# Gated attention and MLP, one decode step: 512 columns of a weight row moved onto the first six DMA engines, the bias loaded once, and two weight matrices interleaved on TensorE

## The chip, the core and the metric

The kernel runs on one core of a Trainium2 chip. The metric is device time in microseconds (us) for one execution; the time before is the median of three runs. The profile is one further execution that the hardware profiler recorded. In it PE is TensorE's matmul side and PEld its weight loads, DVE is VectorE, ACT is ScalarE, POOL is GpSimd, and SP is SyncE, which here only issues DMAs.

## What is computed

```
g = sigmoid((x * gate_w).sum(-1))                      # x: 2 rows of 576
q = x @ wq                                             # 32 heads of 128
a = softmax(q . k_cache / sqrt(128)) . v_cache  @ wo   # 4096 keys per head; wo: 4096 x 576
b = gelu(x @ w1 + b1) @ w2 + b2                        # w1: 576 x 4608, w2: 4608 x 576
out = g * a + (1 - g) * b
```

All of it is float32. The two caches are 2 x 32 x 4096 x 128 each; with the weights the kernel reads 308.59 MB and writes 4.6 KB.

## The kernel before

**Stages.** First wq and w1 are loaded and multiplied with x (L288 `proj`). Then come 16 steps (L584), each over four heads of one batch row: one 8.4 MB tile of K and one of V. DVE multiplies K by q and sums (L506, L511, L512; POOL helps at L510), ACT takes the exponential (L531), TensorE multiplies with V (L545). At the end come w2 and wo, which TensorE multiplies into one PSUM tile `acc` (L367), and for the last nine rows of wo into `res` (L457, L481); ACT and DVE copy the result out (L477, L486) and SP stores it (L487).

**The ring and the DMA queue.** One SBUF tile `ring` holds three slots of 16384 columns (64 KB per partition). SP issues K, V and the closing weights strictly in the order of `seq` (L100 to L104). A load goes out as soon as the slot that it overwrites is free, so that the DMA engines have work queued nearly all the time. DMAs take eight completion semaphores in turn, so each one also waits until the DMA eight places ahead of it has landed.

**The closing weights.** `LAST` (L66) lists three slots: w2 rows 0 to 27; w2 rows 28 to 35, the piece `wx`, and wo rows 0 to 15; wo rows 16 to 31. "Row r" of w2 here means one of 36 rows that each partition holds (576 columns, 2304 bytes per partition). wo has 32 such rows and goes out in ever smaller DMAs, so that little is left to multiply after the last one.

**The piece wx.** Row 35 of w2 isn't loaded whole over 128 partitions. Its last 288 columns (`DS`) are left out of the w2 DMA (L158), and come through four small DMAs (L155) whose outer dimension is 4 rows (`XE` = 4) with 8 segments of 288 columns each. They put 128 segments into 16 partitions. The matching 128 entries of the hidden vector are spread in the same way with eight tiny matmuls against the identity (L411) into `hx`, and `mlp_x` (L417) multiplies these segments with eight matmuls of 16 rows.

**acc.** Its 576 output columns are two halves of 288 that sit at different partitions (L363 `acc_mm`). [...]

**The bias.** b1 is loaded by ACT's queue into a zeroed tile at two rows of each of four partition groups, one per batch row: the first copy in one DMA early (L221), the second in five pieces after the wq product (L315). The sum at L390 adds it to the hidden row.

**The end.** L601 to L623 write out the order: softmax and attention of the last step, mixed with `mlp_out` (w2), the normalisation (`norm_sum`, `norm_t`, `o_turn`), `mlp_x`, the remaining w2 rows, `wo_out(0, FOLD)` for wo rows 0 to 22 and `last_out` for rows 23 to 31.

Of the kernel before, what the change touches and what calls it, by code (L numbers as in the profile page):

```python
# [8 lines left out]
F32 = mybir.dt.float32  # L9
# [3 lines left out]
P = 128  # L13
# [6 lines left out]
def kernel(  # L20
# [14 lines left out]
    nc = tc.nc  # L35
    B, H, SK, DH = k_cache.shape
    D = x.shape[-1]
# [12 lines left out]
    NG = 4  # L50
# [30 lines left out]
    cp = ctx.enter_context(tc.tile_pool(name="cp", bufs=1))  # L81
# [8 lines left out]
    ps_sm = ctx.enter_context(tc.tile_pool(name="ps_sm", bufs=3, space=bass.MemoryType.PSUM))  # L90
# [8 lines left out]
    kt, vt, wqt, w1t, rows = {}, {}, {}, {}, {}  # L99
# [22 lines left out]
    def slot(n):  # L122
        k = len(held) % SLOTS
        return ring[:, k * SLOT:k * SLOT + n]
# [13 lines left out]
    srcx2 = w2.rearrange("(e c s r) n -> c r e s n", e=XE, c=XC, s=XS)[:, NF - 1, :, :, DS:]  # L138

    def length(w, a, z):  # L140
        return XS * DS if w == "wx" else (z - a) * D - (DS if (w, z) == ("w2", NF) else 0)

    def load_last(m):
        n = sum(length(*q) for q in LAST[m])

        used["e"], used["z"] = len(held) % SLOTS * SLOT + n, (len(held) % SLOTS + 1) * SLOT
        t = slot(n)
        o = 0
        for w, a, z in LAST[m]:
            if w == "wx":  # L150
                xt = t[:XP, o:o + XS * DS]
                rows[w] = xt.rearrange("p (s n) -> p s n", s=XS)
                o += XS * DS
                for c in range(XC):
                    nc.sync.dma_start(xt[c::XC].rearrange("e (s n) -> e s n", s=XS), srcx2[c])  # L155
                continue
            if (w, z) == ("w2", NF):
                nc.sync.dma_start(t[:, o:o + length(w, a, z)], srcs[w][:, a * D:z * D - DS])  # L158
                for r in range(a, z):
                    rows[w, r] = t[:, o + (r - a) * D:o + min((r - a + 1) * D, length(w, a, z))]  # L160
                o += length(w, a, z)
                continue

            ends = (a * D, a * D + DS, a * D + DS + DO, z * D) if (w, z) == ("wo", 32) else (a * D, z * D)
            for u, v in zip(ends, ends[1:]):
                nc.sync.dma_start(t[:, o:o + v - u], srcs[w][:, u:v])
# [41 lines left out]
    b1r = temp(F4)  # L208
# [3 lines left out]
    load()  # L212
    load()

    def load_b1(b, ends):
        to, src = b1r.rearrange("(g q) n -> g q n", g=NG)[:, b], b1.rearrange("(g n) -> g n", g=NG)
        for u, v in zip(ends, ends[1:]):
            nc.scalar.dma_start(to[:, u:v], src[:, u:v])  # L218
# [10 lines left out]
    ident = cp.tile([P, P], F32, name="ident")  # L229
# [9 lines left out]
    for j in range(NPB):  # L239
        t = cp.tile([P, NT * 32 + EB], F32, name=f"p{j}")  # L240
# [86 lines left out]
    for f in range(HG):  # L327
# [10 lines left out]
    nc.vector.tensor_copy(  # L338
        spread.rearrange("p (e c) -> p e c", e=E), row4.unsqueeze(2).to_broadcast([NO, E, PE_])
    )  # L340
    qs = {}
# [20 lines left out]

    def acc_mm(lhsT, rhs, k, start=False, stop=False, lo=0):  # L363
        m = lhsT.shape[-1]
        for s in range(lo, lo + rhs.shape[-1] // DS):
            o = 64 * (k % 2) + 32 * s
            nc.tensor.matmul(  # L367
                acc[o:o + m], lhsT, rhs[:, (s - lo) * DS:(s - lo + 1) * DS], start=start, stop=stop, skip_group_check=True
            )

    g1z = cp.tile([1, 2, 32], F32, name="g1z")
    nc.gpsimd.memset(g1z, 0.0)
# [26 lines left out]
    nc.vector.tensor_mul(t, hb, hb)  # L399
# [6 lines left out]

    load()

    hxps = ps_sm.tile([XP, XS, B], F32, tag="sm", name="hxps")
    for s in range(XS):  # L410
        nc.tensor.matmul(  # L411
            hxps[:, s], ident.rearrange("p (q s) -> p s q", s=XS)[:, s], hg[:, NF - 1], start=True, stop=True
        )
    hx = cp.tile([XP, XS, B], F32, name="hx")
    nc.scalar.copy(hx, hxps)

    def mlp_x():  # L417
        for s in range(XS):
            acc_mm(hx[:, s], rows["wx"][:, s], s, lo=1)

    def mlp_out(lo, hi):
        for r in range(lo, hi):
            acc_mm(hg[:, r], rows["w2", r], r)
# [4 lines left out]
    oP = cp.tile([P, B, 32], F32, name="oP")  # L428

    def o_turn(turn):  # L430
        t = late(B * 32).rearrange("p (b c) -> p b c", c=32)
        for b in range(B):
            nc.vector.transpose(t[:, b], oT[:, b])
        ps = ps_sm.tile([P, B * 32], F32, tag="sm", name="op_t")
        nc.tensor.matmul(ps, turn, t.rearrange("p b c -> p (b c)"), start=True, stop=True)
        nc.vector.tensor_copy(oP.rearrange("p b c -> p (b c)"), ps)

    def wo_out(lo, hi):
        for r in range(lo, hi):
            acc_mm(oP[:, :, r], rows["wo", r], r)  # L440
# [127 lines left out]
    def norm_sum():  # L568
        sums = ps_sm.tile([NO, 1], F32, tag="sm", name="psum")
        nc.tensor.matmul(sums, rs, ones, start=True, stop=True)  # L570
        f = late(1, NO)
        nc.vector.reciprocal(f, sums)
        nc.vector.tensor_mul(f, f, gall)
        nc.vector.tensor_reduce(osum, oall.rearrange("p (r d) -> p d r", d=DH), AX.X, ALU.add)
        nc.vector.tensor_scalar_mul(osum, osum, f[:, 0:1])

    def norm_t():
        ps = ps_sm.tile([P, NO], F32, tag="sm", name="oT_t")
        nc.tensor.transpose(ps, osum, ident[:NO, :NO])
        nc.vector.tensor_copy(  # L580
            oT.rearrange("p b (h e) -> p h b e", e=E), ps.rearrange("p (h b e) -> p h b e", b=B, e=E)
        )

# [68 lines left out]
```

## Time and profile before

| what | value |
|---|---|
| median of three runs | 721.72 us (721.49 to 721.81) |
| the profiled execution | 721.61 us, of which the span from first to last instruction is 719.7 us |
| DMA queue of SP, share of 16 engines over the span | 99.2% |
| DVE busy | 511.8 us (71%) |
| PE busy | 216.2 us (30%) |
| ACT busy / POOL busy | 40.0 us / 145.0 us |

The view of windows gives for each stretch of time the busy time of each engine with the number of its instructions, the granted TensorE clock, and the share of the time in which the 16 DMA engines were busy with packets that began in that stretch; in a short stretch a long packet can push that share above 1. The chain of waits follows the work that ended last backwards. The timeline has start, duration, engine, line, operation, tiles, shapes and count, and in square brackets how long the engine stood idle before and on whom it waited.

### The profile page before, as it was taken

How to read it: one execution, taken by the hardware profiler on the slowest of the kernel's cores; microseconds unless marked ns; L12 is line 12 of the kernel's file. 1: busy time of each engine (PE TensorE's matmuls, PEld its weight loads, DVE VectorE, ACT ScalarE, POOL GpSimd, SP SyncE). 2: the span in 40 equal slices, each digit the busy share in tenths (PEclk: the TensorE clock that was granted, in tenths of full speed). 3: DMA queues.
4: the chain of work that ended last, by engine and by line, in shares of the span. 5: the costliest groups of instructions: out<-in, count | busy, mean ns of one | idle time of the engine just before them, and what ended most of it. 6: DMA issues, size and time to landing. Idle time of an engine off the chain costs nothing.

```text
span 719.7 us, 3881 instructions
## 1 busy us (share of the span) xinstructions
PE 216.2 (30%) x1647; PEld 62.6 (9%) x1647; DVE 511.8 (71%) x136; ACT 40.0 (6%) x156; POOL 145.0 (20%) x35
## 2 busy tenths in 40 slices
PE   0665022040515050404032140505050503113195
PEld 0322000010101010101000010101010100000032
DVE  0004969779695969596969879696959695988910
ACT  0110010100001010101010100001010101010000
POOL 2000130404050403022040404040503122040400
PEclk9977556575756575566657575657575665757599
DMA  9999999999999999999999999999999999999997
GB/s 409 412 446 427 423 452 415 459 416 452 423 437 424 444 426 430 442 430 441 433 431 437 430 426 444 427 437 437 437 427 448 419 434 433 430 441 434 417 424 310
DMA packets 7278, 308.85 MB, mean 429 GB/s; under 512 B 830, under 2 KB 1362, under 8 KB 1628
## 3 DMA queue, kind: packets, MB, share of 16 engines
q1 hardware_dynamic: 7204, 308.55, 99.2%
q8 instruction: 13, 0.21, 0.1%
q10 hardware_dynamic: 56, 0.05, 0.0%
q14 instruction: 5, 0.04, 0.0%
HBM read 308.59 MB, written 0.00 MB: 429 GB/s over the span
## 4 chain that ended last, share of the span: by engine, by line
DMA 47%; DVE 35%; PE 15%; ACT 1%; issue 1%; ACTq 1%; POOL 0%; DVEq 0%; SPq 0%; POOLq 0%
DMA ring<-in_A_k_cache_dram 38%; DVE ring L506 19%; DVE s L511 10%; PE av L545 10%; DVE s L512 5%; DMA ring<-in_B_w_dram 4%; DMA ring<-in_A_wo_dram 3%; DMA ring<-in_gate_w_dram 3%; PE oall L562 2%; PE qps L303 2%; PE acc L367 1%; DVE avs L556 1%; ACTq L218 0%; PE qps L328 0%; ACT p L531 0%
## 5 line engine op out<-in xcount | busy, mean ns | idle before, releaser
L506 DVE TENSOR_TENSOR ring<-ring,q 128x16384 f32<-128x16384 f32 x16 | 275.6, 17225 | 109.1 <-DMA ring<-in_A_k_cache_dram 109.1
L510 POOL TENSOR_TENSOR ring<-ring 128x3968 f32<-128x3968 f32 x16 | 137.0, 8565 | 490.1 <-DVE ring L506 490.1
L545 PE MATMUL av<-ring,p 128*32 128x512 f32 x1024 | 137.5, 698 | 166.9 <-ACT p L531 166.9
L511 DVE TENSOR_REDUCE s<-ring 128x66 f32<-128x8448 f32 x16 | 143.3, 8953 | 1.3
L562 PE MATMUL oall<-avs,pick 128*64 128x512 f32 x16 | 14.8, 1028 | 196.7 <-DVE avs L556 168.3
L512 DVE TENSOR_REDUCE s<-ring 128x62 f32<-128x3968 f32 x16 | 68.4, 4277 | 0.1
L545 PEld LDWEIGHTS av<-ring,p 128*32 128x32 f32 x1024 | 35.1, 127 | 274.8 <-issue 217.8
L531 ACT ACTIVATE p<-s,bs 32x128 f32<-32x128 f32 x64 | 25.5, 398 | 478.9 <-DVE bs L525 477.7
L351 PE MATMUL qb<-qm,spread 64*128 64x512 f32 x8 | 8.3, 1138 | 72.5 <-POOL qm L347 72.5
L390 DVE TENSOR_TENSOR ring<-hps,ring 128x384 f32<-128x384 f32 x3 | 1.7, 559 | 33.3 <-PE hps L303 33.1
L562 PEld LDWEIGHTS oall<-avs,pick 128*64 128x64 f32 x16 | 2.2, 196 | 203.5 <-DVE avs L556 203.5
L367 PE MATMUL acc<-ring,hg 128*2 128x288 f32 x142 | 11.9, 487 | 26.1 <-DMA ring<-in_B_w_dram 26.1
L283 DVE TENSOR_SCALAR gb<-gb 128x2 f32<-128x2 f32 x1 | 0.2, 170 | 24.7 <-ACT gb L282 24.7
L556 DVE TENSOR_TENSOR avs<-av,selr 128x512 f32<-128x512 f32 x8 | 5.5, 682 | 10.6 <-PE av L545 10.6
L303 PE MATMUL hps<-ring 128*32 128x384 f32 x120 | 12.8, 598 | 0.0
L347 POOL TENSOR_TENSOR qm<-qall,mine 64x512 f32<-64x512 f32 x4 | 4.1, 1032 | 41.7 <-ACT qall L330 41.7
L477 DVE COPY ring<-res 2x144 f32<-2x144 f32 x1 | 0.3, 297 | 16.4 <-PE res L457 16.4
L531 ACT ACTIVATION_READ_ACCUMULATOR p<-s,bs 32x1 f32 x64 | 11.8, 184 | 0.0
L303 PE MATMUL qps<-ring 128*32 128x512 f32 x80 | 11.3, 729 | 0.0
L270 PE MATMUL xps<-ident,ring 3*128 3x3 f32 x10 | 1.5, 254 | 24.0 <-DMA ring<-in_gate_w_dram 23.1
L351 PEld LDWEIGHTS qb<-qm,spread 64*128 64x128 f32 x8 | 2.0, 307 | 75.6 <-POOL qm L347 75.6
L353 ACT COPY q<-qb 128x512 f32<-128x512 f32 x4 | 2.3, 586 | 106.3 <-PE qb L351 106.3
(87 smaller groups left out, 74.3 us busy)
## 6 DMA issues: line engine op xcount, KB each, us to landing
ring<-in_B_w_dram SPq DMA_DIRECT2D x2, 4608.0 KB, 34.4
ring<-in_B_w_dram SPq DMA_DIRECT2D x2, 4032.0 KB
ring<-in_A_wo_dram SPq DMA_DIRECT2D x2, 2304.0 KB, 14.9
ring<-in_B_w_dram SPq DMA_DIRECT2D x1, 2160.0 KB
ring<-in_A_wo_dram SPq DMA_DIRECT2D x1, 2016.0 KB
ring<-in_B_w_dram SPq DMA_DIRECT2D x1, 1152.0 KB, 14.7
ring<-in_A_wo_dram SPq DMA_DIRECT2D x1, 1152.0 KB
ring<-in_A_wq_dram SPq DMA_DIRECT2D x1, 1024.0 KB
```

Of the source, the lines that this page charges most:

```text
L303: nc.tensor.matmul(ps[32 * j:32 * j + 32, :width], lhs, ts[c][:, o:o + width], start=(k == 0), stop=last, skip_group_check=True,)
L347: nc.gpsimd.tensor_mul(t, qall.unsqueeze(1).to_broadcast([NO, NQ, DH]), mine[:, u[0]:u[-1] + 1].unsqueeze(2).to_broadcast([NO, NQ, DH]),)
L351: nc.tensor.matmul(ps, spread, t.rearrange("p u d -> p (u d)"), start=True, stop=True)
L367: nc.tensor.matmul(acc[o:o + m], lhsT, rhs[:, (s - lo) * DS:(s - lo + 1) * DS], start=start, stop=stop, skip_group_check=True)
L506: nc.vector.tensor_mul(kt[i], kt[i], qs[i].unsqueeze(1).to_broadcast([P, R, DH]))
L510: nc.gpsimd.tensor_add(t[:, :, :DH2], t[:, :, :DH2], t[:, :, DH2:])
L511: nc.vector.tensor_reduce(st[i][:, HALVED:], kt[i][:, HALVED:], AX.X, ALU.add)
L512: nc.vector.tensor_reduce(st[i][:, :HALVED], t[:, :, :DH2], AX.X, ALU.add)
L531: nc.scalar.activation(p[w, :, e * RB:(e + 1) * RB], st[i][w].rearrange("p (t c) -> p t c", c=RB), AF.Exp, bias=bias[i][w], accum_out=rs[w ...
L545: nc.tensor.matmul(ps[32 * j:32 * j + 32], p[:, 32 * t + EB * (1 - half):32 * t + EB * (1 - half) + 32], vt[i][:, RB * t:RB * (t + 1)].rea ...
L556: nc.vector.tensor_mul(t, avs[i].rearrange("p (r d) -> p r d", d=DH), selr.unsqueeze(2).to_broadcast([P, RB, DH]))
L562: nc.tensor.matmul(oall, pick[:, NO - G - i * G:2 * NO - G - i * G], avs[i].rearrange("p r d -> p (r d)"), start=(i == 0), stop=(i == N // ...
```

## The change

Six edits:

1. wx grows from 288 to 512 columns of row 35 of w2 and is cut for six rows instead of four: four DMAs of 6 x 5 segments (120 segments, 24 partitions), and a fifth DMA of 4 x 2 segments for the remaining eight. The w2 DMA gets shorter by 224 columns: 4096 instead of 4320 per partition.
2. `hx` becomes two tiles, made by five and two matmuls. A segment of 512 columns crosses the border of the two halves of `acc`, so `acc_mm` cuts it into 224 and 288 columns: 14 matmuls instead of 8.
3. wo is divided between the slots at row 15 instead of 16.
4. Of w2's rows 28 to 35, seven are multiplied later: rows 29 and 30 after wo row 7, rows 31 to 35 after wo row 14.
5. b1 is loaded once, to a third row of each group, one piece early and two pieces later; a new DVE addition after the transposition gives it to both batch rows.
6. Four small operations (the copy to `spread`, the scaling of `osum`, the copies to `oT` and `oP`) go from DVE to ACT.

```
-        (("w2", 28, 36), ("wx", 0, 1), ("wo", 0, 8), ("wo", 8, 16)),
-        (("wo", 16, 23), ("wo", 23, 27), ("wo", 27, 30), ("wo", 30, 31), ("wo", 31, 32)),
+        (("w2", 28, 36), ("wx", 0, 1), ("wo", 0, 8), ("wo", 8, 15)),
+        (("wo", 15, 23), ("wo", 23, 27), ("wo", 27, 30), ("wo", 30, 31), ("wo", 31, 32)),
...
-    XE, XC = 4, 4
+    XE, XC, XS, XW = 6, 4, 5, 512
     XP = XE * XC
-    XS = P // XP
+    XN = XP * XS
+    XR, XT = 4, (P - XN) // 4
+    XL = D - XW
...
                 for c in range(XC):
                     nc.sync.dma_start(xt[c::XC].rearrange("e (s n) -> e s n", s=XS), srcx2[c])
+                yt = t[:XR, o:o + XT * XW].rearrange("p (s n) -> p s n", s=XT)
+                nc.sync.dma_start(yt, srcw[XN:].rearrange("(p s) n -> p s n", s=XT))
...
-    load_b1(0, (0, F4))
+    load_b1(0, 1)
...
-    load_b1(1, (0, 232, 464, 696, 928, F4))
+    load_b1(1, FB)
...
-        for s in range(lo, lo + rhs.shape[-1] // DS):
+        hi = lo + rhs.shape[-1]
+        for s in range(NS):
             o = 64 * (k % 2) + 32 * s
+            u, v = max(lo, s * DS), min(hi, (s + 1) * DS)
...
-    hb = ht[:, :, :B]
+    hb = temp(NF * B).rearrange("p (r b) -> p r b", b=B)
+    nc.vector.tensor_add(hb, ht[:, :, :B], ht[:, :, B:B + 1].to_broadcast([P, NF, B]))
...
-    mlp_out(28, NF)
-    wo_out(0, FOLD)
+    mlp_out(28, 29)
+    wo_out(0, 8)
+    mlp_out(29, 31)
+    wo_out(8, 15)
+    mlp_out(31, NF)
+    wo_out(15, FOLD)
```

In the changed file the same code stands 2 to 21 lines further down: the w2 DMA of L158 is L166 there, wx L155 is L157, the other closing loads L166 are L174, `acc` L367 is L380, `res` L457 is L474.

This is SP's queue near its end, first before and then after, with the semaphores that each DMA waits for (DMAHW0 to DMAHW7 are the eight completion semaphores). The shapes are partitions x columns; 4x8x288 is wx, 128x4608 eight rows of wo.

```order
L158 DMA ring<-in_B_w_dram 128x4320 [waits DMAHW5_49,DVE_49]
L155 DMA ring<-in_B_w_dram 4x8x288 [waits DMAHW6_49]
L155 DMA ring<-in_B_w_dram 4x8x288 x3
L166 DMA ring<-in_A_wo_dram 128x4608
L166 DMA ring<-in_A_wo_dram 128x4608 [waits DMAHW7_49]
L166 DMA ring<-in_A_wo_dram 128x4032 [waits DMAHW0_49,PE_49]
L166 DMA ring<-in_A_wo_dram 128x2304 [waits DMAHW1_49,PE_49]
```

And after:

```order
L166 DMA ring<-in_B_w_dram 128x4096 [waits DMAHW2_49,DVE_49]
L157 DMA ring<-in_B_w_dram 6x5x512 x4
L160 DMA ring<-in_B_w_dram 4x2x512 [waits DMAHW3_49]
L174 DMA ring<-in_A_wo_dram 128x4608 [waits DMAHW4_49]
L174 DMA ring<-in_A_wo_dram 128x4032 [waits DMAHW5_49]
L174 DMA ring<-in_A_wo_dram 128x4608 [waits DMAHW6_49,PE_49]
L174 DMA ring<-in_A_wo_dram 128x2304 [waits DMAHW7_49,PE_49]
```

One DMA more stands ahead of wo, so every wo DMA now waits for a DMA one place later than before: the second wo DMA, which waited for w2's first load, waits for its second; the third, for w2's rows 28 to 35.

This is TensorE from the transposition of `osum` to the first rows that go to `res`, before and after (`hg` marks rows of w2, `oP` rows of wo, `hx` the piece wx; "2x288 x16" are eight rows). Of the fourteen wx matmuls after, the last two are shown.

```order
L579 MATMUL oT_t<-ident,ring 128x64
L367 MATMUL acc<-ring,hx 2x288 x8
L435 MATMUL op_t<-ring 128x64
L367 MATMUL acc<-ring,hg 2x288 x15
L367 MATMUL acc<-ring,oP 2x288 x46
L457 MATMUL res<-ring,oP 2x144 x16
```

```order
L380 MATMUL acc<-ring,hx_328 2x224
L380 MATMUL acc<-ring,hx_328 2x288
L452 MATMUL op_t<-ring 128x64
L380 MATMUL acc<-ring,hg 2x288 x2
L380 MATMUL acc<-ring,oP 2x288 x16
L380 MATMUL acc<-ring,hg 2x288 x4
L380 MATMUL acc<-ring,oP 2x288 x14
L380 MATMUL acc<-ring,hg 2x288 x8
L380 MATMUL acc<-ring,hg 2x64
L380 MATMUL acc<-ring,oP 2x288 x16
L474 MATMUL res<-ring,oP 2x144 x16
```

The fifteen w2 matmuls that stood ahead of all of wo are now 2, 4 and 9, the last with 64 columns, and `op_t` stands behind six more wx matmuls.

More of the change, by code (lines that the diff above doesn't have):

```diff
@@ L146, in load_last @@
         used["e"], used["z"] = len(held) % SLOTS * SLOT + n, (len(held) % SLOTS + 1) * SLOT
+        assert n <= SLOT
         t = slot(n)
@@ L150, in load_last @@
             if w == "wx":
-                xt = t[:XP, o:o + XS * DS]
-                rows[w] = xt.rearrange("p (s n) -> p s n", s=XS)
-                o += XS * DS
+                xt = t[:XP, o:o + XS * XW]
                 for c in range(XC):
                     nc.sync.dma_start(xt[c::XC].rearrange("e (s n) -> e s n", s=XS), srcx2[c])
+                o += XS * XW
+                yt = t[:XR, o:o + XT * XW].rearrange("p (s n) -> p s n", s=XT)
+                nc.sync.dma_start(yt, srcw[XN:].rearrange("(p s) n -> p s n", s=XT))
+                o += XT * XW
+                xt = xt.rearrange("p (s n) -> p s n", s=XS)
+                rows[w] = [xt[:, s] for s in range(XS)] + [yt[:, s] for s in range(XT)]
                 continue
             if (w, z) == ("w2", NF):
-                nc.sync.dma_start(t[:, o:o + length(w, a, z)], srcs[w][:, a * D:z * D - DS])
+                nc.sync.dma_start(t[:, o:o + length(w, a, z)], srcs[w][:, a * D:z * D - XW])
                 for r in range(a, z):
@@ L213, with load_b1 @@
     load()
[L215 to L218, printed above, removed]
-    load_b1(0, (0, F4))
+    def load_b1(lo, hi):
+        for m in range(lo, hi):
+            nc.scalar.dma_start(
+                b1r.rearrange("(g q) n -> g q n", g=NG)[:, B, m * FC:(m + 1) * FC],
+                b1.rearrange("(g n) -> g n", g=NG)[:, m * FC:(m + 1) * FC],
+            )
+    load_b1(0, 1)
     for b in range(B):
@@ L337 @@
     spread = cp.tile([NO, P], F32, name="spread")
-    nc.vector.tensor_copy(
+    nc.scalar.copy(
         spread.rearrange("p (e c) -> p e c", e=E), row4.unsqueeze(2).to_broadcast([NO, E, PE_])
@@ L364, in acc_mm @@
         m = lhsT.shape[-1]
-        for s in range(lo, lo + rhs.shape[-1] // DS):
+        hi = lo + rhs.shape[-1]
+        for s in range(NS):
             o = 64 * (k % 2) + 32 * s
-            nc.tensor.matmul(
-                acc[o:o + m], lhsT, rhs[:, (s - lo) * DS:(s - lo + 1) * DS], start=start, stop=stop, skip_group_check=True
-            )
+            u, v = max(lo, s * DS), min(hi, (s + 1) * DS)
+            if u < v:
+                nc.tensor.matmul(
+                    acc[o:o + m, u - s * DS:v - s * DS], lhsT, rhs[:, u - lo:v - lo],
+                    start=start, stop=stop, skip_group_check=True,
+                )
     g1z = cp.tile([1, 2, 32], F32, name="g1z")
@@ L407 @@
     load()
[L409 to L415, printed above, removed]
+    hx = []
+    for n, lo, m in ((XP, 0, XS), (XR, XN, XT)):
+        ps = ps_sm.tile([n, m, B], F32, tag="sm", name=f"hxps{lo}")
+        to_x = ident[:, lo:lo + n * m].rearrange("p (q s) -> p s q", s=m)
+        for s in range(m):
+            nc.tensor.matmul(ps[:, s], to_x[:, s], hg[:, NF - 1], start=True, stop=True)
+        t = cp.tile([n, m, B], F32, name=f"hx{lo}")
+        nc.scalar.copy(t, ps)
+        hx += [t[:, s] for s in range(m)]
     def mlp_x():
-        for s in range(XS):
-            acc_mm(hx[:, s], rows["wx"][:, s], s, lo=1)
+        for s in range(XS + XT):
+            acc_mm(hx[s], rows["wx"][s], s, lo=XL)
     def mlp_out(lo, hi):
@@ L435, in o_turn @@
         nc.tensor.matmul(ps, turn, t.rearrange("p b c -> p (b c)"), start=True, stop=True)
-        nc.vector.tensor_copy(oP.rearrange("p b c -> p (b c)"), ps)
+        nc.scalar.copy(oP.rearrange("p b c -> p (b c)"), ps)
     def wo_out(lo, hi):
@@ L574, in norm_sum @@
         nc.vector.tensor_reduce(osum, oall.rearrange("p (r d) -> p d r", d=DH), AX.X, ALU.add)
-        nc.vector.tensor_scalar_mul(osum, osum, f[:, 0:1])
+        nc.scalar.mul(osum, osum, f[:, 0:1])
     def norm_t():
@@ L579, in norm_t @@
         nc.tensor.transpose(ps, osum, ident[:NO, :NO])
-        nc.vector.tensor_copy(
+        nc.scalar.copy(
             oT.rearrange("p b (h e) -> p h b e", e=E), ps.rearrange("p (h b e) -> p h b e", b=B, e=E)
```

5 lines of the change are left out of this document (3 added, 2 removed).

## The prediction

> **What bounds the kernel now.** I read the page first, then the view of windows, then the chain of waits and the timeline of the end.
>
> ```profile
> span 719.7 us, 3881 instructions
> DMA packets 7278, 308.85 MB, mean 429 GB/s; under 512 B 830, under 2 KB 1362, under 8 KB 1628
> q1 hardware_dynamic: 7204, 308.55, 99.2%
> q8 instruction: 13, 0.21, 0.1%
> q10 hardware_dynamic: 56, 0.05, 0.0%
> ```
>
> One queue, SP's (q1), keeps the 16 DMA engines busy for 99.2% of the span. No other engine is near that. The windows show where the remaining share goes (the last two columns are the DMA share and GB/s):
>
> ```profile
> 30.00:60.00 30.00, 24.48 (x178) 8.49 (x174) 0.00 (x0) 3.01 (x13) 1.12 (x2) 0.77 1.01 436
> 60.00:680.00 620.00, 154.68 (x1048) 38.57 (x1040) 504.38 (x113) 31.57 (x125) 140.01 (x19) 0.62 1.00 433
> 680.00:712.00 32.00, 27.61 (x317) 9.46 (x319) 5.05 (x13) 2.39 (x9) 0.00 (x0) 0.92 0.99 424
> 712.00:713.50 1.50, 0.87 (x16) 0.27 (x14) 0.00 (x0) 0.40 (x1) 0.00 (x0) 1.00 0.96 391
> 713.50:714.00 0.50, 0.50 (x24) 0.44 (x20) 0.00 (x0) 0.00 (x0) 0.00 (x0) 1.00 0.95 374
> 714.00:714.50 0.50, 0.50 (x24) 0.35 (x16) 0.00 (x0) 0.00 (x0) 0.00 (x0) 1.00 0.78 303
> 714.50:715.00 0.50, 0.22 (x8) 0.00 (x0) 0.00 (x0) 0.00 (x0) 0.00 (x0) 1.00 0.59 214
> 715.00:715.50 0.50, 0.14 (x8) 0.13 (x11) 0.00 (x0) 0.00 (x0) 0.00 (x0) 1.00 0.52 194
> 715.50:716.00 0.50, 0.50 (x24) 0.40 (x16) 0.00 (x0) 0.00 (x0) 0.00 (x0) 1.00 0.46 158
> 716.00:716.50 0.50, 0.50 (x22) 0.17 (x12) 0.00 (x0) 0.00 (x0) 0.00 (x0) 1.00 0.47 119
> 716.50:717.00 0.50, 0.50 (x15) 0.24 (x12) 0.10 (x1) 0.06 (x1) 0.00 (x0) 1.00 0.00 0
> ```
>
> From 30 to 712 us the share stays at 0.99 to 1.01: no gap is there to close. The end is ragged: in engines out of 16 the shares are 15.2, 12.5, 9.4, 8.3, 7.4, 7.5, then none. So about four engines have finished by 714.5, four more by some 715, and eight carry the rest to about 716.5. The unused part from 713.5 to 716.5 is (0.05 + 0.22 + 0.41 + 0.48 + 0.54 + 0.53) x 0.5 = 1.1 us of all sixteen. That is what perfect levelling of the same bytes would give.
>
> ```profile
> 695.27 20.04 DMA ring<-in_A_wo_dram
> 715.31 0.04 issue
> 715.36 1.56 PE res L457 x36
> 716.92 0.28 DVE ring L477
> ```
>
> The chain says the same: 20 us of wo transfers, then TensorE takes up the last rows as they land, and copies follow. TensorE itself waits for DMA at each piece:
>
> ```profile
> 697.79 2.10 PE L367 MATMUL acc<-ring,hx 16*2 16x288 f32 x16
> 699.82 0.43 PE L435 MATMUL op_t<-ring 128*128 128x64 f32 x2
> 705.82 2.12 PE L367 MATMUL acc<-ring,oP 128*2 128x288 f32 x32 [1.58 <-DMA ring<-in_A_wo_dram]
> 710.57 2.11 PE L367 MATMUL acc<-ring,oP 128*2 128x288 f32 x28 [2.63 <-DMA ring<-in_A_wo_dram]
> 712.73 0.40 ACT L446 COPY ring<-acc 128x288 f32<-128x288 f32 x1 [17.24 <-PE acc L367]
> 714.29 0.43 PE L467 MATMUL res<-ring,fold 128*2 128x144 f32 x8
> 716.67 0.48 PE L481 MATMUL res<-ring,oP 128*2 128x72 f32 x8
> ```
>
> The last matmuls end at 717.15, and 2.55 us of copying and storing stand behind them to the end of the span at 719.7. So the time is the last engine's last byte plus a fixed tail. The question is only how many bytes the last engine carries.
>
> **The transfers.** 433 GB/s over 16 engines are 27.1 GB/s for one, or 27.1 KB per us. The w2 DMA shrinks by 224 columns: 8 partitions x 224 x 4 = 7168 bytes less on each of the 16 engines, 0.26 us. In exchange wx grows. Before, it was 4 DMAs of 8 segments x 1152 bytes per engine, 36.9 KB or 1.36 us on four engines. After, it is 4 x 5 x 2048 = 41.0 KB (1.51 us) on six engines, and 4.1 KB more (0.15 us) on the first four. Net of the w2 part: engines 0 to 3 get 8.2 KB more in wx and 7.2 KB less in w2, +0.04 us; engines 4 and 5, +1.51 - 0.26 = +1.25 us; engines 6 to 15, -0.26 us. The bias takes 4.6 KB off each of the four engines that its four-row DMAs use: -0.17 us. Engines 0 to 3 come to -0.13 us.
>
> That a four-row DMA keeps to engines 0 to 3 and a six-row one to engines 0 to 5 I take from the change's own wording; no row says it. What the trace has is that issuing one differs:
>
> ```profile
> L155 SPq DMA_DIRECT2D ring<-in_B_w_dram x4: 618/624/805, 682.5 to 684.7; - x4
> L158 SPq DMA_DIRECT2D ring<-in_B_w_dram x1: 328/328/328, 681.8 to 681.8; - x1
> ```
>
> SP takes 0.62 us for one of 36 KB and 0.33 us for one of 2160 KB. The Trainium skill, "DMA: Bandwidth & Descriptors", section "Why a DMA increments its semaphore by 16 and not by 1", says that a DMA runs on the largest number of engines, up to 16, that divides the outermost dimension on both sides, on the lowest-numbered ones, and that the issuer itself writes the semaphore steps of the others. The longer issue agrees with that; the engine numbers no view here can show.
>
> Which engine ends last? Eight end together. Four may be those with wx, 1.36 us heavier. The others must be late for another reason, and one is in sight:
>
> ```profile
> q1 hardware_dynamic: 1696, 14.77, 87.3%
> q8 instruction: 3, 0.05, 0.5%
> ```
>
> In the window from 680 to 720 us three fetches of TensorE's instructions took 0.5% of 16 engines x 40 us, 3.2 us, thus about 1.07 us each on whichever engine they hit. All the program has 13. So the late eight are, as I read it, four engines with wx and four that were hit more often, and the early eight hold engines 4 and 5. Then the late engines outside wx win 0.26 us and those with wx 0.13 us. I take 0.26, because with or without wx the eight lie within half a microsecond, and q10's 56 packets (six bias DMAs of four rows, each row with a completion packet, make 48 of them) also become 32, all on engines 0 to 3. The bounds: 0.13 us if an engine with wx is the very last, up to 0.5 if small packets count more than their bytes. Engines 4 and 5 at +1.25 us land at some 715.3 to 716.3, still ahead of the last.
>
> The skill has a rule that speaks against this edit. The same page, section "Rules for kernel authors", says to put a dimension that is a multiple of 16 outermost, since a smaller one confines the DMA to that many engines. By it the 262 KB belong on all sixteen, 0.60 us for each, and the change, which confines 115 KB more, would cost time. The shares of 0.59 down to 0.47 decide against it here: bytes on an engine that is already idle at 715 cost nothing.
>
> **The extra DMA and the later waits.** One more DMA means about 0.6 us more of SP, and the wait one place later:
>
> ```profile
> 682.52 2.83 SPq L155 DMA_DIRECT2D ring<-in_B_w_dram  x4
> 685.40 15.23 SPq L166 DMA_DIRECT2D ring<-in_A_wo_dram  x9
> SPq L166 <- DMA ring<-in_B_w_dram: 8.1, 2, 4.7
> ```
>
> The second wo DMA now waits for w2's second load, as the third did before, and the third for rows 28 to 35; each goes out 4 to 5 us later than before. Queued behind them on SP are the smaller wo pieces only. Cover: wo rows 0 to 7 alone are 147 KB per engine, 5.4 us, and the engines are still on w2 and wx when the second is issued. I cost it at nothing; without that cover an engine would stand up to 4.7 us.
>
> **TensorE's tail.** wx becomes 14 matmuls, 28 records. Bounds: at the pace of the 16 (2.10 us, 0.13 each) 3.7 us, at that of the wo rows (2.12 for 32) 1.9 us. So `op_t` comes up to 1.6 us later, near 701.4, and wo rows 0 to 7 with it. Rows 29 to 35 of w2 are 13 matmuls, 26 records, 1.7 us by the pace of the wo rows, and fall into the idle 1.58 and 2.63 us. The eight rows that now come before row 23 need 32 records, 2.12 us, from about 710.3: `acc` is complete near 712.4, as now. Cover if all this is late: `acc` is needed for L467 at 714.29, the copy ends at 713.13, so 1.2 us are free. Cost 0. On the path: 0.
>
> **ACT, DVE, bias.** One DVE addition more and some copies on another engine:
>
> ```profile
> L399 DVE TENSOR_TENSOR ring<-ring 128x72 f32<-128x72 f32 x1 | 0.2, 235 | 0.0
> L580 DVE COPY oT<-oT_t 128x64 f32<-128x64 f32 x1 | 0.2, 225 | 1.5 <-PE oT_t L579 1.5
> L506 DVE TENSOR_TENSOR ring<-ring,q 128x16384 f32<-128x16384 f32 x16 | 275.6, 17225 | 109.1 <-DMA ring<-in_A_k_cache_dram 109.1
> ```
>
> 0.24 us at 67 us, where DVE waits 109.1 us for K over 16 steps: hidden. The copies at the end lie ahead of wo rows 0 to 7, with the slack above. Three bias DMAs fewer also shift the semaphores of the early loads; at a share of 1.01 there is no gap to close there.
>
> **Sum.** -0.26 us on the last byte, nothing elsewhere: 721.61 - 0.26 = 721.35 for the profiled execution. It lies 0.11 us below the median of the runs shown, so 721.46 by the median; I say 721.4. A measurement of this kernel can tell about 0.2%, 1.44 us, from no change.
>
> **Rivals.**
> - *Better levelling (chance 0.08).* The late engines are just those with wx, and their small packets cost more than I count. For it: eight end together. The ceiling is the 1.1 us above: 720.6. Even that is under 0.2%; with noise 0.03 for more.
> - *Engines 4 and 5 are not early (0.10).* For it: no view names an engine. Against it: by the shares, if the four with wx are among the late eight, eight of the other twelve have finished by some 715. If one of them is among the eight, it ends 1.25 us after the present last: 722.9, or 723.2 with 0.3 us for packets. It is what the skill's rule above would come to.
> - *The six rows do not spread over six engines (0.05).* This is the one that ends slower. If two engines take a six-row DMA, they carry 123 KB of wx instead of 41, +3.0 us on engines that are among the last: 721.6 - 0.1 + 3.0 = 724.5; on three, +1.5 and 723.0. It decides, against 0.2%, where one of the last engines gets 39 KB (1.44 us) more than now. For it: this trace holds no six-row DMA. Against it: the four-row ones, which the rows show going by without trouble, differ in nothing but the count.
> - *An instruction fetch at the end (0.05).* The last one lies in the window from 716 to 717:
>
> ```profile
> q8 instruction: 1, 0.02, 8.9%
> ```
>
> TensorE's stream is 5 matmuls longer ahead of the tail (6 more for wx, one less for `hx`), so that fetch comes some 0.4 us earlier (ten of the 36 records in the 1.56 us of the chain) and could hit an engine that still carries wo: +1.07 - 0.26, 722.4.
>
> **How the numbers follow.** The forecast has 0.72, its own range 720.9 to 721.7. The range 720.6 to 722.8 takes in better levelling, the fetch and most of the forecast's noise; it leaves out late engines 4 and 5 and the worse spread, 0.15. Faster by over 0.2% (below 720.28): 0.03. Slower (above 723.16): six rows on two engines (0.04) and the dear end of late engines 4 and 5 (0.03), 0.07. The rest, 0.90, is no change.
>
> **What would show it.** Right: the shares from 713.5 to 716.5 fuller, about ten engines busy at 715, none after 716.3; L481 starting near 716.4; the 2.55 us behind it unchanged. Idle time of TensorE ahead of the wo pieces near 0 at rows 8 to 14. Wrong: a share of 0.1 to 0.4 that reaches beyond 717 (a few engines overloaded: two or three engines for the rivals with six rows), a share well under 1 between 695 and 712 (the later waits), or L446 starting after 713.9 (TensorE).

## The result and the profile after

The changed kernel took 723.06 us (median of 20 executions, 721.92 to 723.71), the kernel before 721.56 us beside it (20 executions, 721.41 to 722.33). The ratio is 1.0020 with a 95% interval of 1.0014 to 1.0026: slower by 1.0 to 1.9 us. The executions of before lie within 0.9 us, those of after over 1.8 us. That spread is part of the answer, so below the times of a kernel are given as a distribution as well as by a median. One single execution of 994 us, of the kernel with the old bias and row 35 on four engines, is left out.

The profiled execution of after took 723.66 us, 2.05 us more than that of before. Its page still has one queue that is busy all the time, with the smaller bias traffic on q10:

```profile
span 721.7 us, 3898 instructions
q1 hardware_dynamic: 7216, 308.55, 99.1%
q8 instruction: 13, 0.21, 0.1%
q10 hardware_dynamic: 32, 0.03, 0.0%
```

The windows of the end (the last two columns are the DMA share and GB/s):

```profile
714.00:714.50 0.50, 0.50 (x12) 0.06 (x4) 0.00 (x0) 0.00 (x0) 0.00 (x0) 1.00 1.00 401
714.50:715.00 0.50, 0.12 (x4) 0.00 (x0) 0.00 (x0) 0.31 (x1) 0.00 (x0) 1.00 0.77 311
715.00:715.50 0.50, 0.26 (x11) 0.23 (x15) 0.00 (x0) 0.09 (x1) 0.00 (x0) 1.00 0.83 325
715.50:716.00 0.50, 0.50 (x28) 0.43 (x20) 0.00 (x0) 0.00 (x0) 0.00 (x0) 1.00 0.69 259
716.00:716.50 0.50, 0.50 (x24) 0.29 (x12) 0.00 (x0) 0.00 (x0) 0.00 (x0) 1.00 0.64 224
716.50:717.00 0.50, 0.14 (x8) 0.00 (x0) 0.00 (x0) 0.00 (x0) 0.00 (x0) 1.00 0.45 150
717.00:717.50 0.50, 0.21 (x8) 0.20 (x12) 0.00 (x0) 0.00 (x0) 0.00 (x0) 1.00 0.23 83
717.50:718.00 0.50, 0.50 (x24) 0.35 (x18) 0.00 (x0) 0.00 (x0) 0.00 (x0) 1.00 0.18 58
718.00:718.50 0.50, 0.50 (x19) 0.23 (x12) 0.00 (x0) 0.00 (x0) 0.00 (x0) 1.00 0.06 17
```

Two things are to be seen. The fall begins later: at 714.0 to 714.5 the share is 1.00 where before had 0.78, so all engines are late, not only the last. And it ends in a tail: 0.45, 0.23, 0.18 and 0.06 in engines are 7, 4, 3 and 1, where before kept 7.5 engines until 716.5 and then none. TensorE, ScalarE's copy of `acc` and the chain follow the last byte as before (the fourteen matmuls of wx are 28 records, two for each, as the eight of before were 16):

```profile
698.74 2.10 PE L380 MATMUL acc<-ring,hx 24*2 24x224 f32 x28
706.60 3.26 PE L380 MATMUL acc<-ring,oP 128*2 128x288 f32 x26 [2.10 <-DMA ring<-in_A_wo_dram]
712.50 2.12 PE L380 MATMUL acc<-ring,oP 128*2 128x288 f32 x32 [1.13 <-DMA ring<-in_A_wo_dram]
718.60 0.48 PE L498 MATMUL res<-ring,oP 128*2 128x72 f32 x8
```

```profile
714.69 0.40 ACT L463 COPY ring<-acc 128x288 f32<-128x288 f32 x1 [13.23 <-PE acc L380]
```

```profile
697.31 19.93 DMA ring<-in_A_wo_dram
717.24 0.04 issue
717.29 1.55 PE res L474 x36
718.84 0.28 DVE ring L494
```

The last matmuls end at 719.08, and 2.6 us of copying and storing stand behind them, as they did (2.55 us). All 2.05 us were therefore lost by the DMA engines before 719. When, the group of the K multiplications shows, since nearly each of them waits for the last engine of its K tile. First and last start stand in the row; this is before and then after:

```profile
L506 DVE TENSOR_TENSOR ring<-ring,q x16: 17224/17226/17226, 70.4 to 651.1; 128x16384 f32<-128x16384 f32 x16
```

```profile
L523 DVE TENSOR_TENSOR ring<-ring,q x16: 17208/17225/17226, 74.0 to 652.0; 128x16384 f32<-128x16384 f32 x16
```

The last K tile is complete 0.9 us later, before row 35 or any of wo is loaded. So some of the loss arises ahead of it, and the rest of the 2.05 us shows only at the end. The early part is visible on ScalarE. Its timeline around the bias, before and then after (ACTq is ACT issuing DMAs; in brackets its idle time and what ended it):

```profile
39.79 2.65 ACTq L218 DMA_DIRECT2D ring<-in_B_b_dram  x5
42.49 0.89 ACT L322 COPY ring<-ident 128x8 f32<-128x8 f32 x8 [2.36 <-issue]
```

```profile
38.61 1.05 ACTq L226 DMA_DIRECT2D ring<-in_B_b_dram  x2
47.51 0.90 ACT L332 COPY ring<-ident 128x8 f32<-128x8 f32 x8 [8.56 <-DMA ring<-in_B_b_dram]
```

The two late bias pieces are issued 1.2 us earlier than the five, but ScalarE now stands idle for 8.56 us ahead of the eight small copies behind them, until these pieces have landed. In the program's order the wait is there in after and not in before, where it stood on the activation of the hidden vector (L402), at a place where the bias had long come:

```
before  L322 COPY ring<-ident 128x4x2 [waits Pool_49]
before  L402 ACTIVATE ring<-ring 128x72 [waits DMAHW2_49,DMAHW3_49,DMAHW1_49,DMAHW4_49,DMAHW0_49,DVE_49]
after   L332 COPY ring<-ident 128x4x2 [waits DMAHW1_49,DMAHW0_49,Pool_49]
after   L417 ACTIVATE ring<-ring 128x72 [waits DVE_49]
```

The copies neither read nor write the bias; why the program puts the wait there I can't say from the runs. On the copies hangs TensorE's query product, behind that, on the same engine, the product with w1, and on that the slot that V's first tile overwrites. SP's issue of that V tile and its wait, before and then after:

```profile
61.43 0.33 SPq L130 DMA_DIRECT2D ring<-in_A_v_cache_dram  x1
SPq L130 <- PE hps L303: 13.3, 1, 13.3
```

```profile
66.07 0.33 SPq L130 DMA_DIRECT2D ring<-in_A_v_cache_dram  x1
SPq L130 <- PE hps L313: 18.0, 1, 18.0
```

V goes out 4.6 us later. That matters because of what is queued ahead of it. By the completion events in the trace the sixteen engines finish the first K tile from 68.4 to 70.2 us, in both kernels. Before, the next 8.4 MB had been queued 7.0 us ahead of the first of these times; after, 2.4 us ahead. And the V tile's completions, as a mean over the engines, follow those of K after 19.32 us before and after 19.75 us after. So the engines were without queued work for 0.43 us each in the mean. The shares of the windows can't show it, since at this place they count 64 KB packets by their start.

### The profile page after: what moved, and what is told of

Its sections match the earlier page's. It is cut to its first block, busy times and chain, and to the rows that moved or that the text cites. A ratio compares the mean times of both kernels' runs of the same rounds, so it can differ in the third digit from the quotient of the medians.

```text
span 721.7 us, 3898 instructions
## 1 busy us (share of the span) xinstructions
PE 218.4 (30%) x1657; PEld 64.1 (9%) x1657; DVE 510.9 (71%) x133; ACT 41.1 (6%) x161; POOL 145.0 (20%) x35
## 4 chain that ended last, share of the span: by engine, by line
DMA 47%; DVE 35%; PE 14%; ACT 2%; issue 1%; ACTq 0%; POOL 0%; SPq 0%; DVEq 0%; POOLq 0%
DMA ring<-in_A_k_cache_dram 39%; DVE ring L523 19%; DVE s L528 10%; PE av L562 9%; DVE s L529 5%; DMA ring<-in_A_wo_dram 3%; DMA ring<-in_gate_w_dram 3%; ACT p L548 2%; DMA ring<-in_B_w_dram 2%; PE hps L313 2%; PE qps L313 1%; DMA ring<-in_B_b_dram 1%; PE qps L338 1%; PE zps L289 0%; DVE ring L409 0%
## 5 line engine op out<-in xcount | busy, mean ns | idle before, releaser
L562 PE MATMUL av<-ring,p 128*32 128x512 f32 x1024 | 139.0, 704 | 161.2 <-ACT p L548 161.2
L529 DVE TENSOR_REDUCE s<-ring 128x62 f32<-128x3968 f32 x16 | 68.4, 4276 | 0.0
L380 PE MATMUL acc<-ring,hg 128*2 128x288 f32 (+1 forms) x142 | 13.6, 505 | 25.8 <-DMA ring<-in_B_w_dram 25.8
L380 PE MATMUL acc<-ring,oP 128*2 128x288 f32 x92 | 8.0, 475 | 3.3 <-DMA ring<-in_A_wo_dram 3.2
```

Source lines behind the costliest of these rows:

```text
L380: nc.tensor.matmul(acc[o:o + m, u - s * DS:v - s * DS], lhsT, rhs[:, u - lo:v - lo], start=start, stop=stop, skip_group_check=True,)
L529: nc.vector.tensor_reduce(st[i][:, :HALVED], t[:, :, :DH2], AX.X, ALU.add)
L562: nc.tensor.matmul(ps[32 * j:32 * j + 32], p[:, 32 * t + EB * (1 - half):32 * t + EB * (1 - half) + 32], vt[i][:, RB * t:RB * (t + 1)].rea ...
```

## The experiments

Theory A: the loss comes from the late bias pieces, by way of ScalarE's copies and V's first load. Rival B: the early shift is hidden, and all the loss is the ragged end. The first four kernels set them against each other.

**Late bias pieces behind the first query unit.**

```
     nc.scalar.dma_start(b2r, b2[None, :])
-    load_b1(1, FB)
...
     q_unit(0)
+    load_b1(1, FB)
```

> The changed kernel with the two late bias pieces issued behind the first q tile instead of ahead of the small ACT copies at L332. Theory A (the late pieces hold ACT for 8.6 us, so the first V tile is issued 4.6 us later and the DMA engines run empty at 68 us; part of the 1.1 us by which the sixteen engines are later on the average): V's first load goes out near 61.5 us again, and the time falls by 0.4 to 1.1 us to 722.0 to 722.7. Theory B (all of the loss is the end: an engine that got wx is a late one): no change, 723.1.

**Row 35 as before, all else changed.**

```
-    XE, XC, XS, XW = 6, 4, 5, 512
+    XE, XC, XS, XW = 4, 4, 8, 288
```

> The changed kernel with wx as before: 288 columns over four engines. Theory A: still 722.0 to 722.7, above before by 0.4 to 1.1 us, with V's first load at 66 us. Theory B: 721.5, as before, since the overloaded engine is gone.

**The kernel before with the bias edit alone.**

```
-    load_b1(0, (0, F4))
+    load_b1(0, 1)
...
-    load_b1(1, (0, 232, 464, 696, 928, F4))
+    load_b1(1, FB)
...
-    hb = ht[:, :, :B]
+    hb = temp(NF * B).rearrange("p (r b) -> p r b", b=B)
+    nc.vector.tensor_add(hb, ht[:, :, :B], ht[:, :, B:B + 1].to_broadcast([P, NF, B]))
```

> The kernel before with the bias edit alone (one copy, one early piece and two late ones, the addition after the transposition). Theory A: ACT waits some 8 us at L324 and the time rises by 0.4 to 1.1 us, to 722.0 to 722.7. Theory B: 721.5, no change.

**The changed kernel with the bias as before** (the reverse of that diff).

> The changed kernel with the bias loaded as before. Theory A: the time falls by 0.4 to 1.1 us from 723.1, to 722.0 to 722.7, what is left being the end; V's first load near 61.5 us. Theory B: no change, 723.1.

Here are all runs of ten executions or more, these and the later ones; those with fewer come further down. The mean of before beside them was 721.59 to 721.64 throughout, and none of its executions was above 722.34.

```
kernel                                 executions  above 722.4  median   mean    ratio to before (95%)
after                                      20          18       723.06  723.05   1.0020 (1.0014 to 1.0026)
after, late bias behind query unit         11           5       721.60  722.12   1.0007 (0.9998 to 1.0016)
after, row 35 on four                      11           8       723.13  722.85   1.0017 (1.0008 to 1.0026)
before, bias edit alone                    11           5       722.29  722.43   1.0012 (1.0003 to 1.0021)
after, bias as before                      11           6       722.62  722.23   1.0009 (1.0000 to 1.0018)
after, late bias, row 35 on four           11           0       721.74  721.80   1.0002 (0.9993 to 1.0011)
after, old bias, row 35 on four            10           0       721.60  721.64   1.0000 (0.9991 to 1.0009)
before, row 35 on six alone                11           6       722.63  722.30   1.0009 (1.0000 to 1.0018)
after, bias whole and early                11           4       722.02  722.15   1.0007 (0.9998 to 1.0016)
before, five engines, 384 columns          11           2       721.60  721.79   1.0003 (0.9994 to 1.0012)
before, four engines, 384 columns          11           1       721.69  721.81   1.0003 (0.9994 to 1.0012)
before, six engines, 256 columns           11           1       722.06  722.04   1.0006 (0.9997 to 1.0015)
after, late bias, five engines, 384        11           0       721.65  721.70   1.0001 (0.9992 to 1.0010)
```

B falls: with row 35 as before the loss stays (723.13), and the bias edit by itself costs 0.80 us in the mean. A holds as far as it goes; its 722.0 to 722.7 misses two of the four medians, 721.60 with the late bias and 723.13 with row 35 on four. In the run with the late bias behind the query unit ScalarE does not wait and V goes out at 55.5, with 12.9 us in hand instead of 2.4:

```profile
39.72 0.90 ACT L331 COPY ring<-ident 128x8 f32<-128x8 f32 x8
55.54 0.33 SPq L130 DMA_DIRECT2D ring<-in_A_v_cache_dram  x1
L523 DVE TENSOR_TENSOR ring<-ring,q x16: 17224/17226/17227, 70.0 to 650.9; 128x16384 f32<-128x16384 f32 x16
```

In the one with the bias edit alone both come back:

```profile
48.00 0.90 ACT L324 COPY ring<-ident 128x8 f32<-128x8 f32 x8 [8.59 <-DMA ring<-in_B_b_dram]
64.87 0.33 SPq L130 DMA_DIRECT2D ring<-in_A_v_cache_dram  x1
```

That profiled execution had 3.4 us in hand; its V tile followed after 19.33 us, nothing lost, and it took 721.62 us. The one with row 35 on four engines had 2.4 us in hand (issued at 65.92), followed after 19.93 us and took 723.23. So by these three profiles the edge lies between 2.4 and 3.4 us of lead. The times of the bias edit alone spread from 721.62 to 723.61, as they would if its executions fall on both sides of that edge; no profile shows one of its long ones.

The profile with row 35 on four engines answers one thing more. Its end has a tail like that of after:

```profile
716.50:717.00 0.50, 0.50 (x24) 0.29 (x20) 0.00 (x0) 0.00 (x0) 0.00 (x0) 1.00 0.27 95
717.00:717.50 0.50, 0.50 (x24) 0.42 (x24) 0.00 (x0) 0.00 (x0) 0.00 (x0) 1.00 0.16 53
718.00:718.50 0.50, 0.50 (x16) 0.28 (x12) 0.04 (x1) 0.00 (x0) 0.00 (x0) 1.00 0.12 34
```

Its last load's completions spread over 4.23 us, those of after over 4.18, of before over 3.22. So the tail goes with the late V load and is no sign of the six engines. How a mean loss of 0.6 us at 88 us becomes 1.5 us on the last engine the trace doesn't tell, since it names no engine.

A is not all, however. With the bias mended in either way about half of the executions are back at 721.2 to 721.9 us, and the other half stand 1.2 to 1.4 us above (by the groups' medians); with the late bias there is nothing between (721.25, 721.41, 721.43, 721.51, 721.59, 721.60 and 722.50, 722.75, 722.90, 722.90, 723.43). ScalarE doesn't wait in either kernel and V goes out early enough (55.5 and 60.0), so it isn't the early shift that makes the second group. Theory C puts it to row 35's 512 columns on six engines, theory D to the rest of the change: the kept-back rows, ScalarE's copies, wo's boundary at 15.

**Late bias behind the query unit and row 35 on four** (both diffs above).

> The changed kernel with the two late bias pieces issued behind the first query unit and with row 35 of w2 as before (288 columns on four engines). Theory A (the loss is V's first load, issued 4.6 us late): as in the run with only the bias moved, most executions at 721.4 to 721.7. The open remainder is a second group of times some 1.2 us higher that the runs with the late bias behind the query unit and with the bias as before both had. Theory C (that group comes from row 35's 512 columns on six engines): no second group here, all times within 721.3 to 722.0 and a median of 721.5. Theory D (it comes from the kept-back rows, the copies on ScalarE or wo's second boundary): the second group stays, with some 3 to 6 of 11 times at 722.4 or above.

**Bias and row 35 as before; the order, the copies and the boundary changed.**

> The changed kernel with the bias as before in six pieces and row 35 of w2 as before: what is left of the change is the order of rows 29 to 35 behind wo's rows 7 and 14, the copies moved to ScalarE and wo's boundary at row 15. Theory C: one group of times, 721.3 to 722.0, median 721.5. Theory D: a second group of times at 722.4 to 723.0 with some 3 to 6 of 11 times.

**The kernel before with row 35 on six engines and wo's boundary at 15** (these parts of the change's diff alone).

> The kernel before with row 35's 512 columns of w2 on six engines and wo's boundary at row 15, everything else (bias, order on TensorE, copies on VectorE) as before. Theory C: two groups of times, some 5 of 11 at 722.4 to 723.0 and the others at 721.3 to 722.0. Theory D: one group at 721.3 to 722.0. By my prediction's levelling alone it would be 0.1 to 0.3 us faster than before.

**The changed kernel with the bias loaded once, whole and early.**

```
-    load_b1(0, 1)
+    nc.scalar.dma_start(
+        b1r.rearrange("(g q) n -> g q n", g=NG)[:, B], b1.rearrange("(g n) -> g n", g=NG)
+    )
...
-    load_b1(1, FB)
```

> The changed kernel with the bias loaded once and whole, early, in one DMA at the place of the first piece, so that nothing late is left for ScalarE's eight copies to wait for. Theory A: V's first load is issued at 61.5 us or earlier and no engine runs dry at 68 us; the lower group of times at 721.3 to 721.6. Theory B (all of the loss is at the end): 722.4 to 723.4 as in the changed kernel. Theory C and D both leave a second group at 722.4 to 723.0 here, since the six engines, the order and the copies are all in it.

C holds and D falls: without the six engines there is no second group (21 executions, though two of those with the late bias reach 722.03 and 722.30), with them there is, in all four kernels. The bias whole and early is the least clear of these, with 722.02 and 722.11 between the groups; its V load goes out at 55.7 us. What is left of the change when bias and row 35 are put back (kept-back rows, copies, boundary) costs nothing: 721.60 against 721.58. Added to before one by one, the two costs make up the whole: the bias edit alone has a mean of 0.80 us above before, the six engines alone of 0.66 us, the whole change of 1.44 us. Taken out of the change one by one, they are 0.93 and 0.20 us. A mean of eleven is uncertain by some 0.25 us, so the runs don't tell these two accounts apart, and the close sum is partly luck.

Why half of the executions? Two more runs of the kernel with row 35 on six were meant to catch a profile of the second group.

> The kernel before with only row 35's 512 columns on six engines, once more, for a profile of the higher group of its times. Two accounts of that group. Theory E (an engine with a piece of row 35 is a late one in such an execution): in a profile at 722.6 or above the DMA share falls below 1 from 714 us on and 0.1 to 0.4 of it lasts until 717 us, as in the changed kernel, while the loads up to 690 us end within 0.2 us of the lower group's. Theory F (all engines are late, by longer packets somewhere): the stages before 690 us end 1 us later and the share at the end falls as steeply as in the lower group, only later.

> As the run before this one; the higher group held 6 of its 11 times, so one of two should show it. Theory E: share of 0.1 to 0.4 until 717 us or later. Theory F: a steep end, later by some 1 us.

Both fell into the lower group (721.56 and 721.39 us), so no profile shows the second group undisturbed by the bias, and E against F was not settled in this way. Two other kernels changed the count of engines and the width.

**Five engines, 400 columns; and four engines, 432 columns** (the first in the kernel before with wo's boundary at 15, the second with the order and copies of after too).

```
-    XE, XC, XS, XW = 6, 4, 5, 512
+    XE, XC, XS, XW = 5, 4, 6, 400
```

```
-    XE, XC, XS, XW = 4, 4, 8, 288
+    XE, XC, XS, XW = 4, 4, 8, 432
```

> The kernel before with 400 columns of row 35 on five engines instead of 288 on four, and wo's boundary at row 15. If it is the fifth engine that is late in the higher group, that group stays here, some 1.0 us above the lower one, with about half of the times; if only the sixth is, there is one group at 721.3 to 722.0. Theory F (longer packets everywhere, nothing to do with which engine) has one group here or two without regard to the count of engines.

> The changed kernel with the bias as before and 432 columns of row 35 on the first four engines, so that these four carry half as much again as before and no fifth or sixth engine carries any. Theory E: one group of times and no second one at +1.2 us, since the four are never late; the four early engines get 144 columns x 32 rows x 4 bytes or 18 KB more each, which their lead of some 1.5 us before row 35 takes up: 721.3 to 722.2. If it is the width of row 35's part and not the engine that makes the second group, it stays.

They took 730.64 and 725.67 us (medians of four and five executions), as nothing had led me to expect, and said nothing on the question. With these widths SP got a new wait ahead of row 35, for loads that were still running (the row of the five engines, then that of the four):

```profile
SPq L157 <- DMA ring<-in_B_w_dram: 11.9, 1, 11.9
694.00:696.00 2.00, 2.00 (x35) 0.93 (x37) 1.19 (x4) 0.00 (x0) 0.00 (x0) 1.00 0.00 0
```

```profile
SPq L157 <- DMA ring<-in_B_w_dram: 7.0, 1, 7.0
694.00:696.00 2.00, 2.00 (x26) 0.85 (x28) 0.86 (x3) 0.43 (x1) 0.00 (x0) 1.00 0.05 20
```

For 2 us the DMA engines have nothing or next to nothing to do. Widths of 256, 288, 384 and 512 columns don't bring this wait, so the next kernels keep to those.

They test an account (theory G) that came from the trace's records; theory H stands for the other accounts, by the width of the piece or by its form. The records of q8, TensorE's instruction fetches, have durations that repeat with a period of eight. In the kernel with six engines: 926, 960, 962, 949, 880, 880, 944, 938 ns, then 921, 961, 967, 953. I read this as eight engines taken in turn. The completion times of one load's sixteen parts fit that. Those of the load at 687 us, after ten fetches, make groups of 8, 6 and 2 (us after the first):

```
0.00 0.21 0.22 0.58 0.68 0.72 0.76 0.94 | 1.22 1.27 1.35 1.36 1.43 1.47 | 2.85 2.92
```

By that reading eight engines were hit by no fetch, six by one and two by two. The last two stand clearly apart; the border between the eight and the six (0.94 and 1.22) is drawn to fit the count. By the means of the groups a fetch would cost its engine 0.8 to 1.5 us. By the end there were twelve, hence four engines hit once and four twice. If row 35's engines lie outside the eight, then by their completions in the last load three sorts are left: never hit and without row 35, hit once, and all the rest. The first two sorts count 4 and 4 with four engines (before), but with six engines 3 and 3:

```
before      0.00 0.44 0.71 0.86 | 1.48 1.56 1.57 1.59 | 2.33 and later
six engines 0.00 0.23 0.27      | 1.39 1.44 1.51      | 2.23 and later
```

Three left unhit means that only five of the six with row 35 are outside the eight. The sixth is one of the eight; here it had been hit once. In an execution in which it is one of the four that are hit twice it would end some 1.3 us later, and that would be half of them, if the turn began at each of the eight with equal chance.

The other profiles bear the counts out: 3 and 3 also in the five others with 512 columns on six engines and no wait for the bias (in two of them with a less clear border behind the second 3), 4 and 4 in the four others with 288 or 384 columns on four engines in which V lost nothing. The equal chance they don't bear out. The first durations (934, 926, 884, 879 ns) are places in the same series of eight, and by them the eighteen profiles begin at only four of the eight places. From each of these four the engine behind that of 947 ns (880 to 888 ns) is hit once by the twelfth fetch. If that is the sixth, it explains why all seven profiles with six engines and no wait for the bias are of the lower group. After begins at the same place as before and as two of these seven. That the turn begins elsewhere in the executions that are not profiled is not shown.

**Five engines with 384 columns, four with 384, six with 256** (in the kernel before, boundary at 15).

```
-    XE, XC, XS, XW = 6, 4, 5, 512
+    XE, XC, XS, XW = 5, 4, 6, 384
```

> The kernel before with 384 columns of row 35 on five engines, and wo's boundary at row 15; no added wait on SyncE. Theory G: if the sixth engine is the one that also brings instructions, one group of times, 721.3 to 722.0; if the fifth is, two groups some 1.2 us apart as with six engines. Theory H: two groups, or one, whatever the engine, as in the run with four engines of 384 columns.

> The kernel before with 384 columns of row 35 on four engines, and wo's boundary at row 15. An engine with 32 rows of 1536 bytes has some 2.1 us for them by the records of 1152 (51 ns) and 2048 bytes (84 ns), 0.4 us more than with 288 columns, which these four early engines can take. Theory G: one group, 721.3 to 722.0. Theory H by width: a second group some 0.6 us higher; H by the form in 24 and 4 rows: one group.

> The kernel before with 256 columns of row 35 on six engines, and wo's boundary at row 15. Theory G: the engine that is hit twice has 20 rows of 1 KB (some 47 ns each, 1.0 us) instead of 20 of 2 KB (1.7 us) to bear, so the second group stays but lies only some 0.5 us above the lower one. Theory H by width: no second group; H by form: the second group at 1.2 us above as before.

G's forecasts come out but for a few strays. With six engines and 256 columns there are two groups that lie closer, 721.56 to 721.79 (five) and 722.06 to 722.35 (five, and one at 723.17): their medians are 0.63 us apart, where some 0.5 was expected and 1.2 had been measured with 512 columns. With five engines nine of eleven lie at 721.40 to 721.83, with four and the same width ten of eleven at 721.63 to 721.80, so it is the sixth engine that brings the second group, and the width sets how far off it lies. Five engines have the fifth DMA and the later waits of wo too, so these don't make the group either. The last loads agree: five engines leave 3 unhit and 4 hit once (0.00 0.22 0.40 | 1.52 1.67 1.72 1.83 | 1.97 and later). Two and one stray executions at 722.7 to 722.9, where the second group would be, stay unexplained. What is shown is that the sixth engine costs the time in about half of the executions; that instruction fetches are the reason is argued from the records and from these forecasts, and no profile shows it at work.

**Both causes mended:** the changed kernel with the late bias behind the query unit, and 384 columns on five engines.

> The changed kernel with the late bias pieces issued behind the first query unit and with 384 columns of row 35 on five engines; the kept-back rows, the copies on ScalarE and wo's boundary at row 15 stay as changed. If the two causes are all of the loss: one group of times at 721.3 to 721.8 with at most a stray one above, a median of 721.4 to 721.7, no measurable difference from before. If something else of the change costs time: a median of 722.0 or more, or a second group. That it is faster than before by over 0.2% (720.2 or less) neither account expects.

721.65 us, one group of 721.33 to 722.06: no difference from before that can be measured (0.9992 to 1.0010). So the two causes account for the loss as far as the runs can tell, and what is left of the change brings nothing. No version beat the kernel before.

## Why the prediction was wrong

- **The bias edit, costed as hidden.** This is the step that failed: "Three bias DMAs fewer also shift the semaphores of the early loads; at a share of 1.01 there is no gap to close there". It looked for a gain and at SP's semaphores. It left out ScalarE, on whose own queue the late pieces are issued: the wait for them moved from L402, where it was free, ahead of the eight copies, and the query product, w1's product and V's first load are queued behind these. A share of 1.01 says that no gap is there; it doesn't say how much delay the queue bears. That was 7.0 us of lead, and 4.6 us of it went. Measured: +0.80 us in the mean for the bias edit alone (1.0003 to 1.0021).
- **Engines 4 and 5 as early ones.** The rival "Engines 4 and 5 are not early", with a chance of 0.10 and 722.9 us, came true for one engine and in about half of the executions: the upper group of the kernels without the bias cost lies around 722.7 to 722.9 (medians of four kernels). That the whole change came out near this number, at 723.06, is chance, since there the bias cost is in it. I had counted late engines in one profile, and, if theory G is right, in one profile the fetches' turn begins at one place. The mean cost was +0.66 us. A DMA with six rows does run on six engines: each of the four has six completions in the trace, which lie within 0.7 us where row 35 alone was changed. The rival with two or three engines falls.
- **The gain of 0.26 us.** The lower group with six engines has a median of 721.55 us, five engines with 384 columns 721.60, before 721.6. By these medians levelling has brought 0.1 us at most; where the rest of the 0.26 us went no run tells.
- **The rule that I weighed against the trace.** The Trainium skill, "DMA: Bandwidth & Descriptors", section "Rules for kernel authors", advises against an outermost dimension below 16. I set it aside since bytes on an idle engine cost nothing. With four or five engines that held (1.0003 for either with 384 columns); with six it did not (+0.66 us), by theory G since the sixth is not an early engine in each execution.
- **What was right.** The tail behind the last matmul stayed at 2.6 us. The 28 records of wx took 2.10 us, near the lower of the two bounds. The kept-back rows, ScalarE's copies and the boundary at 15 cost nothing (1.0000, 0.9991 to 1.0009), and with the later waits of wo the kernel with both causes mended has no loss either (1.0001, 0.9992 to 1.0010). The second wo load went out 4.5 us later, near the 4 to 5 forecast, the third 6.7 us. That TensorE would hardly wait ahead of rows 8 to 14 did not come true: it waited 2.10 us there. Of the signs named for a wrong forecast two were there: a share of 0.1 to 0.4 reaching beyond 717, and the copy of `acc` starting after 713.9, at 714.69. The first was to mean a few overloaded engines, but the kernel with row 35 on four engines has it too. The second only shifted with the rest, by 1.96 of the 2.05 us, and the chain doesn't pass through it.

The early shift and the sixth engine don't explain every tenth. By the trace the engines of after lose another 0.3 us in each of two stretches between 185 and 225 us, where its 64 KB packets take 2.45 and 2.44 us in the mean instead of 2.42, and the change with row 35 on four engines has a mean 0.42 us above that of the bias edit alone, about as much as the two means of eleven are uncertain. That stays open.

## What to carry to other kernels

Where one DMA queue is the bound, ask of each edit by how much it shifts the issue of the next large load, on every engine in the chain ahead of it, and hold that against the lead that the load has over the first engine that runs out of work. A change to the DMAs that an engine issues can move the engine's wait for them, here ahead of instructions that don't use the data. And which DMA engines are the early ones can't be taken from one profile: it shows one execution, and here none of seven profiles showed the group of times that about half of the other executions had.

## What the hardware showed

- A lead of 2.4 us from SP's issue of an 8.4 MB load to the first engine's last queued byte was not enough (0.43 and 0.62 us lost per engine); 3.4 us was (two profiles and one). The issue itself takes 0.33 us, so by estimate some 2 to 3 us more pass before the engines have the new work.
- TensorE's 16 KB instruction fetches, 13 in the program, have records of some 0.9 us. Read from their durations and the completion times, which name no engine, they go round eight of the sixteen engines, cost the one they hit 0.8 to 1.5 us each, and begin at one of four places in the eighteen profiles. What the page gives as a share of 0.1% thus seems to put the engines 2.9 us apart by 687 us.
- Where two small DMAs of ScalarE (6 KB each, at 39 us) are issued moved the mean of a 720 us kernel by 0.93 us: 723.05 ahead of the eight copies, 722.12 behind the first query unit.
